# One SBUF offset for weights and tokens, and half of a head pair's scaled states on another engine

## The chip, the cores and the metric

The kernel runs on one core of a Trainium2 chip. The metric is the device time of one execution in microseconds (us). Engines are named as in the profile: PE is TensorE (matmul), PEld its weight load, DVE is VectorE, ACT is ScalarE, POOL is GpSimd, SP is the engine that issues the DMAs.

## The reference: what is computed

Three stages follow each other: a gated linear attention (4 batches, 8 heads, 768 steps, head size 48), a feed-forward layer 384 to 2048 to 384 with `h * cos(h)`, and one 384 to 768 to 384 with the largest of three products. All in float32.

```
for t in range(S):
    state = alpha[:, :, t, :, None] * state + einsum('bhd,bhe->bhde', k[:, :, t], v[:, :, t])
    y[:, :, t] = einsum('bhd,bhde->bhe', q[:, :, t], state)
x = y, as 3072 tokens x 384
h = x @ moe_w_in;  x = (h * cos(h)) @ moe_w_out
h = max(x @ w1, x @ w2, x @ w3);  out = h @ w_out
```

## The kernel before, in words

**Tiling.** The 3072 tokens are cut into 6 units of 512. Tokens lie along the free axis, features along the partitions. Every weight and every token tile is kept as a high and a low part in the format `float32r`, and each product is three matmuls of 128 x 128 weights on 128 x 512 tokens: high times high, high times low, low times high. In the first layer (`moe1`, L489 to L536) one step is one of 16 blocks of 128 hidden features of one unit: nine matmuls into a PSUM bank `ps` (L497 to L499, weights `wih`, `wil`, tokens `xt`), a chain on ACT and DVE that makes `h * cos(h)` and splits it into `gh` and `gl`, and nine matmuls into the three accumulators `acc` (L524 to L526, weights `woh`, `wol`, tokens `gh`, `gl`). There are 96 steps, so 1728 such matmuls. The second layer has `moe2_h` (L574 to L576, weights `w0h` to `w2l`, tokens `xt`) and `moe2_o` (L597 to L599, weights `wo2h`, `wo2l`, tokens `h`), 1296 matmuls of the same shape.

**Attention** (`att`, L337 to L486) works on one pair of heads and one unit, 24 blocks in all, four a unit. The 512 tokens are eight chunks of 64. Per block: scans on DVE make the decays `g` and `al`, two products on POOL scale k and q (`kq`), PE transposes k (L387), makes the scores and the chunk's state increments (L399, L404), DVE runs through the eight chunks' states `s` (L421, L423), each state is scaled by its decay into `d`, and PE makes the values (L449 from the masked scores `a`, L455 from `d`). So each block puts three pieces of small matmuls between the large ones. In the first unit (`u < DAC`) ACT makes `d`, with one ACTIVATE of 48 x 48 per chunk and head of the pair (L430); in the later units POOL does, one TENSOR_TENSOR of 48 x 384 per head (L435).

**Weights.** Each of 32 blocks of the first layer passes through a `raw` buffer (three of them): a DMA, three DVE instructions (L310 to L312), the high part on ACT (L315: `wih`, `woh`), the low part on POOL (L316: `wil`, `wol`). Those of the first layer come in during the first unit.

**The order.** Python records every operation with an engine, an estimated duration, its dependences and a due time. `Program.order` (L118) lays them out on the engines in an imagined run, and picks the PSUM bank of each short-lived tile; the kernel is then issued in that order. Each engine works strictly in its order. So a change of an estimated duration, or of the engine of an operation, moves others on all engines.

**Where tiles lie.** In the built program the token tiles of the first layer (`xt`, `gh`, `gl`) start, within a line of 512 bytes of a partition, at byte 128, and so does each block of 512 or 2048 bytes in them. The first layer's weights are a pool at the other end of SBUF, whose tiles start at byte 480 of such a line. In the second layer `w0h` to `w2l` and `xt` start at byte 128, and `wo2h`, `wo2l` and their tokens `h` at byte 480.

Of the kernel before, what the change touches and what calls it, by code (L numbers as in the profile page):

```python
# [9 lines left out]
F32 = mybir.dt.float32  # L10
# [3 lines left out]
AF = mybir.ActivationFunctionType  # L14
# [4 lines left out]
B, H, S, D = 4, 8, 768, 48  # L19
# [4 lines left out]
P = 128  # L24
C = 64
HB = 512
NC = HB // C
# [4 lines left out]
C1 = C + 1  # L32
AL = NC * C1
N2 = NC // 2
KO = AL + 2
# [5 lines left out]
PR = 112  # L41
# [6 lines left out]


NQ, NG, NRAW, NIN, NV, NGS = 3, 2, 3, 3, 2, 3  # L50
NBANK = 5
LIMIT = {"h": 3, "a": 3, "t": 1, "w": 1, "r": 2, "y": 2, "r0": 4}

# [9 lines left out]
MKP = 1  # L63

DAC = 1


W1E = 10
# [10 lines left out]
class Program:  # L79
# [15 lines left out]
    def op(self, eng, dur, fn, reads=(), writes=(), due=0.0, nbytes=None, port=False):  # L95
        n = len(self.ops)
        deps = set()
        for k in reads:
            if k in self.last_write:
                deps.add(self.last_write[k])  # L100
        for k in writes:
            if k in self.last_write:
                deps.add(self.last_write[k])
            deps.update(self.readers.get(k, ()))
        for k in writes:
            self.last_write[k] = n
            self.readers[k] = []
        for k in reads:
            self.readers.setdefault(k, []).append(n)
        for k in {*reads, *writes}:  # L110
            if isinstance(k, tuple) and k[0] == "ps":
                self.of_bank.setdefault(k, []).append(n)
        deps.discard(n)
        port = port or (eng == "Pool" and nbytes is None)
        self.ops.append((eng, dur, nbytes, fn, sorted(deps), due, port))
        return n
# [89 lines left out]
def act(n, psum=False):  # L206
    return (0.05 if psum else 0.095) + 0.00084 * n
# [6 lines left out]
def pool(n):  # L214
    return 0.16 + 0.0021 * n
# [25 lines left out]
def tile_kernel(ctx, tc, qka, vv, wt, outT):  # L241
    nc = tc.nc
    ve, se, ge, pe = nc.vector, nc.scalar, nc.gpsimd, nc.tensor
# [11 lines left out]
    wp = s_w1.enter_context(tc.tile_pool(name="w1p", bufs=1, side="right"))  # L255
    ap = s_at.enter_context(tc.tile_pool(name="ap", bufs=1))
# [3 lines left out]
    wi = {n: wp.tile([P, NF1, NR, P], F32R, name=f"wi{n}") for n in "hl"}  # L260
    wo = {n: wp.tile([P, NF1, DM], F32R, name=f"wo{n}") for n in "hl"}

    q_b = [mp.tile([P, HB], F32, name=f"q{i}") for i in range(NQ)]
    gh_b = [mp.tile([P, HB], F32R, name=f"gh{i}") for i in range(NG)]
    gl_b = [mp.tile([P, HB], F32R, name=f"gl{i}") for i in range(NG)]
# [2 lines left out]
    acc = [pp.tile([P, HB], F32, name=f"acc{i}") for i in range(NR)]  # L268
    ps_b = [pp.tile([P, 512], F32, name=f"ps{i}") for i in range(NBANK)]

    one0 = ap.tile([PR, NC, C1], F32, name="one0")
    inv0 = [ap.tile([PR, NC, C1], F32, name=f"inv{i}") for i in range(2)]
    tri = ap.tile([P, 1, C], F32, name="tri")
    al_b = [ap.tile([PR, KO], F32, name=f"al{i}") for i in range(NIN)]
    kq_b = [ap.tile([PR, 2 * HB], F32, name=f"kq{i}") for i in range(NIN)]
    g_b = [ap.tile([PR, AL], F32, name=f"g{i}") for i in range(NGS)]
    v_b = [ap.tile([P, N2, 2, UP], F32, name=f"v{i}") for i in range(NV)]
    kt_b = [ap.tile([P, N2, PR], F32, name=f"kt{i}") for i in range(2)]
    a_b = [ap.tile([P, 2, N2, C], F32, name=f"a{i}") for i in range(2)]
# [57 lines left out]
    def att(u, k, p, t0):  # L337
        m = u * NP + k
        n, n2 = m % NIN, m % 2
        t, kq_, v, kt, a, s, d, iv = al_b[n], kq_b[n], v_b[m % NV], kt_b[n2], a_b[n2], s_b[p], d_b[n2], inv0[n2]  # L340
# [8 lines left out]
        g = gf.rearrange("p (c t) -> p c t", c=NC)  # L349
# [4 lines left out]
        kg, ik, tk, dk, sk = ("g", m % NGS), ("iv", n2), ("kt", n2), ("d", n2), ("s", p)  # L354
        firsts = [(u * NC + c) % CPB == 0 for c in range(NC)]
# [3 lines left out]
        if u == 0:  # L359
# [13 lines left out]
            kgs = [(*kg, 0), (*kg, 1)]  # L373
        else:
            op("DVE", 0.07 + 0.00208 * AL, lambda: ve.tensor_tensor_scan(
                gf[:, ::-1], t[:, 1:AL + 1][:, ::-1], one0.rearrange("p c t -> p (c t)"), 0.0, ALU.mult, ALU.add), ["one0", kf], [(*kg, 0), (*kg, 1)], t0 - 1, port=True)
            kgs = [(*kg, 0), (*kg, 1)]
# [40 lines left out]
        def state(c):  # L418
            o, kvc = s[:, (c + 1) % NC], r[c % 2][0:PR, c // 2 * D:(c // 2 + 1) * D]
            if firsts[c]:  # L420
                ve.tensor_copy(o, kvc)  # L421
            else:
                ve.scalar_tensor_tensor(o, s[:, c], g[:, c, 0:1], kvc, ALU.mult, ALU.add)  # L423

        for c in range(NC - 1):
            op("DVE", 0.2, lambda c=c: state(c), [rk[c % 2], *kgs, (*sk, c)], [(*sk, c + 1)], t0 + 0.25)
            if u < DAC and not firsts[c + 1]:
                for j in range(2):
                    w = slice(UP * j, UP * j + D)
                    op("Act", act(D) + 0.09, lambda c=c, j=j, w=w: se.activation(d[w, j, c + 1], s[w, c + 1], AF.Copy, scale=g[w, c + 1, 0:1]),  # L430
                       [*kgs, (*sk, c + 1)], [(dk, j, c + 1)], t0 + 0.25)
        if u >= DAC:
            for j in range(2):
                w = slice(UP * j, UP * j + D)
                op("Pool", pool(NC * D), lambda j=j, w=w: ge.tensor_tensor(d[w, j], s[w], g[w, :, 0:1].to_broadcast([D, NC, D]), ALU.mult),  # L435
                   [*kgs, *[(*sk, c) for c in range(NC)]], [(dk, j, c) for c in range(NC)], t0 + 0.25)
        elif not firsts[0]:
            for j in range(2):
                w = slice(UP * j, UP * j + D)
                op("Act", act(D) + 0.09, lambda j=j, w=w: se.activation(d[w, j, 0], s[w, 0], AF.Copy, scale=g[w, 0, 0:1]), [*kgs, (*sk, 0)], [(dk, j, 0)], t0 + 0.25)  # L440
        op("DVE", 0.2, lambda: state(NC - 1), [rk[1], *kgs, (*sk, NC - 1)], [(*sk, 0)], t0 + 0.27)

        yks, y = ([("acc", 0), ("acc", 1)], acc[:2]) if u == 0 else psum2("r" if u <= RYS else "y")
# [103 lines left out]
    def open_np():  # L547
        s_w1.close()
        np_ = ctx.enter_context(tc.tile_pool(name="np", bufs=1, side="right"))
        w2t["h2"] = [np_.tile([P, NF2, 2, HB], F32R, name=f"h2_{i}") for i in range(2)]  # L550
        w2t["t"] = [np_.tile([P, HB], F32, name=f"t2_{i}") for i in range(2)]
        w2t["y"] = [np_.tile([P, HB], F32, name=f"y2_{i}") for i in range(2)]
        for n in "hl":
            w2t["o" + n] = np_.tile([P, NF2, DM], F32R, name=f"wo2{n}")

    def x2_in(u, t0):
        n = u % 2
        for c in range(NR):
            op("SP", HW, lambda c=c: nc.sync.dma_start(x_tile(NU + u).bitcast(F32)[:, c], x1d[u, c]),
               [("x1d", u, c)] + ([("xtA", n)] if c else []),  # L560
               [*halves(n, c), ("xp", n, c, 0), ("xp", n, c, 1)] + ([] if c else [("xtA", n)]), t0, dma(P * HB * 8))
# [44 lines left out]
    def build():  # L606
# [41 lines left out]
        for u in range(NU):  # L648
            for k, p in enumerate((NP - 1, *range(NP - 1))):
                t = FIRST + k if u == 0 else NF1 * (u - 1) + ATT0 + ATTS * k  # L650
                at(t, att, u, k, p, t)
# [19 lines left out]
        x2_in(0, NS - 8)  # L671
        w1k = [(k, f) for k in ("wih", "wil", "woh", "wol") for f in range(NF1)]
        op("SP", 0.0, open_np, (), w1k + ["np"], NS)
        for f in range(NF2):
            weight(NW1 + 3 * NF2 + f, lambda f=f: w2t["oh"][:, f], lambda f=f: w2t["ol"][:, f],
# [13 lines left out]
    build()  # L689
    order, chosen_ = G.order(NBANK, LIMIT)  # L690
    chosen.update(chosen_)
# [68 lines left out]
```

## Time and profile before

| | |
|---|---|
| median of 3 runs | 831.05 us (829.34 to 832.0) |
| the profiled execution | 831.06 us, span of its instructions 829.3 us |
| PE busy | 805.4 us, 97% of the span |
| DVE, ACT, POOL busy | 477.7 us (58%), 372.5 us (45%), 189.0 us (23%) |
| granted TensorE clock, mean over the span | 0.979 |
| chain that ended last | PE 84%, DVE 5%, POOL 4%, issue 3% |

The busy time of PE counts a matmul from its start to its modelled end, and neighbours overlap: a matmul of 128 x 512 is listed with some 400 ns, while the next one starts much sooner. What a matmul costs in a dense stretch is read from the starts, not from that mean.

### The profile page before, as it was taken

Reading aid. Unit: us, or ns where it says so; the run is one execution under the profiler, and the core shown is the slowest. Engines: PE = TensorE matmul, PEld = TensorE weight load, DVE = VectorE, ACT = ScalarE, POOL = GpSimd, SP = SyncE. Lnnn points to the kernel's source line nnn. Section 1 sums busy time; section 2 is a strip of 40 time slices with the busy share of each in tenths; the row PEclk is TensorE's granted clock in tenths of the full one; section 3 lists DMA queues with packets and bytes.
Section 4 is the critical chain, followed back from the end, with each engine's and each line's share of the span. In section 5 each row is a group of like instructions: output and inputs, shape, how many; then the busy total and the mean of one; then the engine's idle time right before and its main releaser. Section 6 shows DMA issues by size and latency. Waiting matters only on the chain.

```text
span 829.3 us, 15144 instructions
## 1 busy us (share of the span) xinstructions
PE 805.4 (97%) x6168; PEld 649.1 (78%) x6168; DVE 477.7 (58%) x924; ACT 372.5 (45%) x695; POOL 189.0 (23%) x187
## 2 busy tenths in 40 slices
PE   7689999999999999999999999999999999999998
PEld 6567777878778877887788778888888888888886
DVE  7689999875786577657679954453122222322221
ACT  5865655645555554556466745521121211112121
POOL 6478777621231023102033200110000000000000
PEclk8589999999999999999999999999999999999999
DMA  9446764330242024102224610232020020200001
GB/s 281 137 133 193 208 188 150 117 106 12 73 146 65 1 76 143 43 1 74 65 86 134 238 45 2 104 106 77 26 88 19 22 89 25 77 26 13 13 26 38
DMA packets 26661, 71.86 MB, mean 87 GB/s; under 512 B 3488, under 2 KB 3488, under 8 KB 26592
## 3 DMA queue, kind: packets, MB, share of 16 engines
q1 hardware_dynamic: 26592, 70.90, 26.9%
q8 instruction: 48, 0.79, 0.4%
q14 instruction: 21, 0.17, 0.1%
HBM read 54.37 MB, written 14.16 MB: 83 GB/s over the span
## 4 chain that ended last, share of the span: by engine, by line
PE 84%; DVE 5%; POOL 4%; issue 3%; DMA 2%; ACT 1%; SPq 0%; DVEq 0%; POOLq 0%; ACTq 0%
PE ps L575 9%; PE ps L576 9%; PE ps L574 9%; PE acc L524 8%; PE acc L526 7%; PE ps L497 7%; PE acc L525 7%; PE ps L499 7%; PE ps L498 7%; PE ps L599 3%; PE ps L598 3%; PE ps L597 3%; PE ps L455 2%; PE ps L449 1%; PE ps L399 1%
## 5 line engine op out<-in xcount | busy, mean ns | idle before, releaser
L497 PE MATMUL ps<-xt,wih 128*128 128x512 f32 x288 | 117.7, 409 | 2.8 <-ACT q L506 1.7
L524 PE MATMUL acc<-gh,woh 128*128 128x512 f32 x288 | 117.5, 408 | 0.3 <-DVE yy L534 0.2
L499 PE MATMUL ps<-xt,wil 128*128 128x512 f32 x288 | 115.0, 399 | 1.4 <-POOL wil L316 1.4
L526 PE MATMUL acc<-gl,woh 128*128 128x512 f32 x288 | 114.4, 397 | 0.6 <-DVE gl L519 0.4
L498 PE MATMUL ps<-xt,wih 128*128 128x512 f32 x288 | 114.8, 399 | 0.0
L525 PE MATMUL acc<-gh,wol 128*128 128x512 f32 x288 | 114.0, 396 | 0.0
L504 ACT ACTIVATE q<-ps 128x512 int32<-128x512 f32 x96 | 57.2, 596 | 70.8 <-PE ps L499 70.2
L584 DVE TENSOR_TENSOR ps<-t,ps 128x512 f32<-128x512 f32 x36 | 25.0, 695 | 104.8 <-PE ps L576 104.7
L513 DVE SCALAR_TENSOR_TENSOR ps<-q,ps 128x512 f32<-128x512 f32 x76 | 52.7, 693 | 55.4 <-ACT q L507 55.2
L506 ACT ACTIVATE q<-q 128x512 f32<-128x512 f32 x96 | 60.6, 631 | 50.3 <-DVE q L505 49.6
L505 DVE SCALAR_TENSOR_TENSOR q<-q,ps 128x512 f32<-128x512 int32 x96 | 65.8, 685 | 28.0 <-ACT q L504 24.8
L585 ACT ACTIVATE h<-ps 128x512 fp32r<-128x512 f32 x36 | 21.5, 598 | 113.1 <-DVE ps L584 113.0
L519 DVE TENSOR_TENSOR gl<-ps,gh 128x512 fp32r<-128x512 f32 x76 | 52.1, 685 | 26.4 <-ACT gh L514 26.2
L497 PEld LDWEIGHTS ps<-xt,wih 128*128 128x128 f32 x288 | 54.6, 189 | 16.2 <-ACT q L506 2.2
L499 PEld LDWEIGHTS ps<-xt,wil 128*128 128x128 f32 x288 | 54.6, 190 | 15.3 <-POOL wil L316 2.1
L524 PEld LDWEIGHTS acc<-gh,woh 128*128 128x128 f32 x288 | 54.2, 188 | 15.0 <-DVE yy L534 1.1
L582 DVE TENSOR_TENSOR t<-t,ps 128x512 f32<-128x512 f32 x36 | 24.7, 687 | 71.4 <-PE ps L576 70.7
L526 PEld LDWEIGHTS acc<-gl,woh 128*128 128x128 f32 x288 | 54.2, 188 | 14.6 <-DVE gl L519 0.8
L514 ACT ACTIVATE gh<-ps 128x512 fp32r<-128x512 f32 x76 | 45.3, 597 | 42.8 <-DVE ps L513 39.9
L498 PEld LDWEIGHTS ps<-xt,wih 128*128 128x128 f32 x288 | 54.8, 190 | 11.8
L525 PEld LDWEIGHTS acc<-gh,wol 128*128 128x128 f32 x288 | 54.3, 189 | 11.7
L435 POOL TENSOR_TENSOR d<-s,g 48x384 f32<-48x384 f32 x40 | 34.6, 864 | 122.7 <-DVE s L423 121.1
(122 smaller groups left out, 1595.2 us busy)
## 6 DMA issues: line engine op xcount, KB each, us to landing
raw<-in_wt SPq DMA_DIRECT2D x56, 384.0 KB, 3.4
kq<-in_qka SPq DMA_DIRECT2D x23, 448.0 KB, 4.5
x1d<-yy SPq DMA_DIRECT2D x18, 512.0 KB, 2.8
xt<-x1d SPq DMA_DIRECT2D x18, 512.0 KB, 4.3
v<-in_vv SPq DMA_DIRECT2D x22, 256.0 KB, 3.5
al<-in_qka SPq DMA_DIRECT2D x24, 228.4 KB, 3.0
outT<-y SPq DMA_DIRECT2D x18, 256.0 KB, 2.0
xt<-yy SPq DMA_DIRECT2D x36, 64.0 KB, 2.7
```

What stands on the lines that cost most here:

```text
L497: pe.matmul(ps, wi["h"][:, f, cc], xt[:, cc, 0], start=(cc == 0), stop=False)
L498: pe.matmul(ps, wi["h"][:, f, cc], xt[:, cc, 1], start=False, stop=False)
L499: pe.matmul(ps, wi["l"][:, f, cc], xt[:, cc, 0], start=False, stop=(cc == NR - 1))
L504: op("Act", act(HB, True), lambda: se.activation(q.bitcast(I32), ps, AF.Copy, scale=INV2PI), [hk], [qk], m)
L505: op("DVE", dve(HB), lambda: ve.scalar_tensor_tensor(q, q.bitcast(I32), -TWOPI, ps, ALU.mult, ALU.add), [hk], [qk], m)
L506: op("Act", act(HB), lambda: se.activation(q, q, AF.Sin, scale=0.5), (), [qk], m)
L524: pe.matmul(acc[c], oh, gh, start=(f == 0), stop=False)
L525: pe.matmul(acc[c], ol, gh, start=False, stop=False)
L526: pe.matmul(acc[c], oh, gl, start=False, stop=(f == NF1 - 1))
L574: pe.matmul(ps, w2t["h"][m][:, f, cc], xt[:, cc, 0], start=(cc == 0), stop=False)
L575: pe.matmul(ps, w2t["h"][m][:, f, cc], xt[:, cc, 1], start=False, stop=False)
L576: pe.matmul(ps, w2t["l"][m][:, f, cc], xt[:, cc, 0], start=False, stop=(cc == NR - 1))
```

## The change

Three things. First, 352 bytes per partition (`pad`, 88 floats) are added at the end of each of the two pools that lie at the upper end of SBUF, so their tiles move down by 352 bytes: the first layer's weights and the second layer's `h` and `wo2` tiles now start at byte 480 - 352 = 128 of a 512 byte line, as the tokens do. Second, attention's tiles `one0`, `inv`, `al` and `g` are allocated with 544 floats (2176 bytes) and used with their old shapes; the `kq` tiles behind them then start at byte 128 instead of 160, and `v`, `a`, `s` and `d` at byte 0 instead of 256. Third, in the first unit ACT scales only the first head's states; the second head's go to POOL, as in the later units, and the estimated duration of the ACT instruction rises by 0.12 us.

```diff
+PAD = 88
+LINE = 544
+DAH = 1
     wo = {n: wp.tile([P, NF1, DM], F32R, name=f"wo{n}") for n in "hl"}
+    wp.tile([P, PAD], F32, name="pad")
...
-    one0 = ap.tile([PR, NC, C1], F32, name="one0")
+    one0 = ap.tile([PR, LINE], F32, name="one0")[:, 0:AL].rearrange("p (c t) -> p c t", c=NC)
-    al_b = [ap.tile([PR, KO], F32, name=f"al{i}") for i in range(NIN)]
+    al_b = [ap.tile([PR, LINE], F32, name=f"al{i}")[:, 0:KO] for i in range(NIN)]
...
             if u < DAC and not firsts[c + 1]:
-                for j in range(2):
+                for j in range(DAH):
-                    op("Act", act(D) + 0.09, lambda c=c, j=j, w=w: se.activation(d[w, j, c + 1], s[w, c + 1], AF.Copy, scale=g[w, c + 1, 0:1]),
+                    op("Act", act(D) + 0.21, lambda c=c, j=j, w=w: se.activation(d[w, j, c + 1], s[w, c + 1], AF.Copy, scale=g[w, c + 1, 0:1]),
-        if u >= DAC:
-            for j in range(2):
+        for j in range(2):
+            if u >= DAC or j >= DAH:
                 op("Pool", pool(NC * D), lambda j=j, w=w: ge.tensor_tensor(d[w, j], s[w], g[w, :, 0:1].to_broadcast([D, NC, D]), ALU.mult),
                    [*kgs, *[(*sk, c) for c in range(NC)]], [(dk, j, c) for c in range(NC)], t0 + 0.25)
...
         for n in "hl":
             w2t["o" + n] = np_.tile([P, NF2, DM], F32R, name=f"wo2{n}")
+        np_.tile([P, PAD], F32, name="pad2")
```

The order changes on all engines from the first unit on. Lines of the changed file stand 4 or 5 below those of before: L430 is L435 there, L435 is L440, L315 is L320, L470 is L474, L475 is L479. The numbers behind a name are tile numbers, one higher in the changed kernel for most tiles.

ACT before, in the first unit, from the second block's values to the third's (`d_125<-s_122` are the scaled states of the third block, `xt` the copies of finished values):

```order
L475 ACTIVATE yy_89<-acc_95 128x256
L430 ACTIVATE d_126<-s_121,g_113 48x48 x3
L411 ACTIVATE a_119<-ps_99 128x256
L411 ACTIVATE a_119<-ps_98 128x256
L430 ACTIVATE d_125<-s_122,g_114 48x48 x8
L470 ACTIVATE xt_463<-acc_94 128x256
L430 ACTIVATE d_125<-s_122,g_114 48x48
L470 ACTIVATE xt_463<-acc_95 128x256
L430 ACTIVATE d_125<-s_122,g_114 48x48
L475 ACTIVATE xt_463<-acc_94 128x256
L430 ACTIVATE d_125<-s_122,g_114 48x48
```

The same place on ACT in the changed kernel:

```order
L479 ACTIVATE yy_90<-acc_96 128x256
L416 ACTIVATE a_120<-ps_100 128x256
L435 ACTIVATE d_126<-s_123,g_115 48x48
L320 ACTIVATE wih<-raw_92 128x384
L435 ACTIVATE d_126<-s_123,g_115 48x48 x2
L320 ACTIVATE woh<-raw_93 128x384
L435 ACTIVATE d_126<-s_123,g_115 48x48
L474 ACTIVATE xt_451<-acc_95 128x256
L474 ACTIVATE xt_451<-acc_96 128x256
L479 ACTIVATE xt_451<-acc_95 128x256
L435 ACTIVATE d_126<-s_123,g_115 48x48
```

Four scaled states instead of eight stand ahead of the first `xt` copy, and the first two weight blocks, which before came after all of the third block's states, now stand among them.

POOL before, from the third block's products to the fourth's masks (`yy` holds the fourth block's k and q):

```order
L367 TENSOR_TENSOR kq_111<-kq_111,g_114 112x512
L412 TENSOR_TENSOR a_120<-a_120,tri 128x256
L382 TENSOR_TENSOR kq_111<-kq_111,al_108 112x512
L412 TENSOR_TENSOR a_120<-a_120,tri 128x256
L412 TENSOR_TENSOR a_119<-a_119,tri 128x256 x2
L367 TENSOR_TENSOR yy_90<-yy_90,g_112 112x512
L316 TENSOR_TENSOR wil<-raw_91,wih 128x384
L382 TENSOR_TENSOR yy_90<-yy_90,al_106 112x512
L412 TENSOR_TENSOR a_120<-a_120,tri 128x256 x2
```

The same place on POOL in the changed kernel:

```order
L372 TENSOR_TENSOR kq_112<-kq_112,g_115 112x512
L440 TENSOR_TENSOR d_126<-s_125,g_113 48x384
L387 TENSOR_TENSOR kq_112<-kq_112,al_109 112x512
L417 TENSOR_TENSOR a_121<-a_121,tri 128x256 x2
L440 TENSOR_TENSOR d_127<-s_122,g_114 48x384
L417 TENSOR_TENSOR a_120<-a_120,tri 128x256 x2
L321 TENSOR_TENSOR wil<-raw_92,wih 128x384
L321 TENSOR_TENSOR wol<-raw_93,woh 128x384
L372 TENSOR_TENSOR yy_91<-yy_91,g_113 112x512
L440 TENSOR_TENSOR d_126<-s_123,g_115 48x384
L387 TENSOR_TENSOR yy_91<-yy_91,al_107 112x512
```

Three of the four new POOL instructions stand here, and the low parts of the first weights are now ahead of the fourth block's first product instead of between its two products.

## Rows read from the trace of the kernel before

**Rows 1.** The page's parts 1 and 2: busy us (share) xinstructions; granted clock.

```profile
PE 805.4 (97%) x6168; PEld 649.1 (78%) x6168; DVE 477.7 (58%) x924; ACT 372.5 (45%) x695; POOL 189.0 (23%) x187
...
PEclk8589999999999999999999999999999999999999
```

**Rows 2.** Windows: stretch, length, busy us of PE, PEld, DVE, ACT, POOL; clock, DMA.

```profile
20.00:40.00 20.00, 13.82 (x199) 10.90 (x199) 12.31 (x34) 16.11 (x49) 8.71 (x9) 0.50 0.50 135
40.00:120.00 80.00, 72.23 (x798) 56.55 (x799) 74.36 (x158) 49.92 (x99) 62.38 (x55) 0.96 0.60 180
130.00:475.00 345.00, 345.00 (x3254) 275.31 (x3255) 254.29 (x503) 197.66 (x354) 89.67 (x86) 1.00 0.29 89
535.00:829.30 294.30, 290.55 (x1275) 238.90 (x1273) 80.55 (x120) 57.51 (x98) 6.10 (x6) 1.00 0.13 47
```

**Rows 3.** Timeline of PE, its last wait in the first unit: start us, us, [idle before].

```profile
129.88 0.50 PE L526 MATMUL acc<-gl,woh 128*128 128x512 f32 x1 [0.26 <-POOL gl L511]
```

**Rows 4.** Timeline of PE, first and last of 121 `moe1` matmuls in a row.

```profile
499.73 0.40 PE L524 MATMUL acc<-gh,woh 128*128 128x512 f32 x1
...
527.84 0.39 PE L574 MATMUL ps<-xt,w1h 128*128 128x512 f32 x1
```

**Rows 5.** Timeline of PE, first and last of 96 `moe2_h` matmuls in a row.

```profile
603.82 0.39 PE L574 MATMUL ps<-xt,w0h 128*128 128x512 f32 x1
...
625.35 0.39 PE L576 MATMUL ps<-xt,w1l 128*128 128x512 f32 x1
```

**Rows 6.** Timeline of PE, starts of three neighbouring runs of matmuls.

```profile
577.00 0.40 PE L597 MATMUL ps<-h,wo2h 128*128 128x512 f32 x1
...
581.14 0.39 PE L574 MATMUL ps<-xt,w2h 128*128 128x512 f32 x1
...
587.30 0.40 PE L597 MATMUL ps<-h,wo2h 128*128 128x512 f32 x1
```

**Rows 7.** Timeline of PE, first and last matmul of the closing stretch.

```profile
535.48 0.40 PE L574 MATMUL ps<-xt,w2h 128*128 128x512 f32 x1
...
825.16 0.39 PE L599 MATMUL ps<-h,wo2h 128*128 128x512 f32 x1
```

**Rows 8.** Groups of PE's instructions from 130 us on: xcount | busy, mean ns | idle.

```profile
L524 PE MATMUL acc<-gh,woh 128*128 128x512 f32 x248 | 100.9, 407 | 0.3 <-DVE yy L534 0.2
...
L497 PE MATMUL ps<-xt,wih 128*128 128x512 f32 x243 | 98.4, 405 | 0.0
```

**Rows 9.** Groups on ACT and POOL, whole span: the scaled states.

```profile
L435 POOL TENSOR_TENSOR d<-s,g 48x384 f32<-48x384 f32 x40 | 34.6, 864 | 122.7 <-DVE s L423 121.1
...
L430 ACT ACTIVATE d<-s,g 48x48 f32<-48x48 f32 x56 | 18.6, 332 | 1.3
```

**Rows 10.** Timeline of ACT, third and fourth block of the first unit.

```profile
24.32 2.83 ACT L430 ACTIVATE d<-s,g 48x48 f32<-48x48 f32 x8
...
30.68 0.56 ACT L315 ACTIVATE wih<-raw 128x384 fp32r<-128x384 f32 x1
...
37.53 4.97 ACT L430 ACTIVATE d<-s,g 48x48 f32<-48x48 f32 x14
```

**Rows 11.** Timeline of POOL, the same stretch.

```profile
27.14 1.18 POOL L367 TENSOR_TENSOR yy<-yy,g 112x512 f32<-112x512 f32 x1 [1.63 <-DVE g L365]
31.31 2.00 POOL L316 TENSOR_TENSOR wil<-raw,wih 128x384 fp32r<-128x384 f32 x1 [2.99 <-ACT wih L315]
33.27 1.17 POOL L382 TENSOR_TENSOR yy<-yy,al 112x512 f32<-112x512 f32 x1
...
38.42 1.01 POOL L316 TENSOR_TENSOR wol<-raw,woh 128x384 fp32r<-128x384 f32 x1
```

**Rows 12.** Timeline of DVE, the same stretch.

```profile
29.08 0.69 DVE L371 TENSOR_TENSOR_SCAN al<-al,acc 112x260 f32<-112x260 f32 x1
...
30.13 2.37 DVE L375 TENSOR_TENSOR_SCAN g<-al,one 112x520 f32<-112x520 f32 x2
36.97 0.21 DVE L421 COPY s<-ps 112x48 f32<-112x48 f32 x1 [4.47 <-ACT a L411]
```

**Rows 13.** Timeline of PE, the fourth block's scores.

```profile
34.50 1.13 PE L399 MATMUL ps<-yy 48*64 48x64 f32 x32 [1.03 <-POOL yy L382]
```

More of the change, by code (lines that the diff above doesn't have):

```diff
@@ L269, in tile_kernel @@
     ps_b = [pp.tile([P, 512], F32, name=f"ps{i}") for i in range(NBANK)]
-    one0 = ap.tile([PR, NC, C1], F32, name="one0")
-    inv0 = [ap.tile([PR, NC, C1], F32, name=f"inv{i}") for i in range(2)]
+    one0 = ap.tile([PR, LINE], F32, name="one0")[:, 0:AL].rearrange("p (c t) -> p c t", c=NC)
+    inv0 = [ap.tile([PR, LINE], F32, name=f"inv{i}")[:, 0:AL].rearrange("p (c t) -> p c t", c=NC) for i in range(2)]
     tri = ap.tile([P, 1, C], F32, name="tri")
-    al_b = [ap.tile([PR, KO], F32, name=f"al{i}") for i in range(NIN)]
+    al_b = [ap.tile([PR, LINE], F32, name=f"al{i}")[:, 0:KO] for i in range(NIN)]
     kq_b = [ap.tile([PR, 2 * HB], F32, name=f"kq{i}") for i in range(NIN)]
-    g_b = [ap.tile([PR, AL], F32, name=f"g{i}") for i in range(NGS)]
+    g_b = [ap.tile([PR, LINE], F32, name=f"g{i}")[:, 0:AL] for i in range(NGS)]
     v_b = [ap.tile([P, N2, 2, UP], F32, name=f"v{i}") for i in range(NV)]
@@ L436, in att @@
                    [*kgs, *[(*sk, c) for c in range(NC)]], [(dk, j, c) for c in range(NC)], t0 + 0.25)
-        elif not firsts[0]:
-            for j in range(2):
+            elif not firsts[0]:
                 w = slice(UP * j, UP * j + D)
-                op("Act", act(D) + 0.09, lambda j=j, w=w: se.activation(d[w, j, 0], s[w, 0], AF.Copy, scale=g[w, 0, 0:1]), [*kgs, (*sk, 0)], [(dk, j, 0)], t0 + 0.25)
+                op("Act", act(D) + 0.21, lambda j=j, w=w: se.activation(d[w, j, 0], s[w, 0], AF.Copy, scale=g[w, 0, 0:1]), [*kgs, (*sk, 0)], [(dk, j, 0)], t0 + 0.25)
         op("DVE", 0.2, lambda: state(NC - 1), [rk[1], *kgs, (*sk, NC - 1)], [(*sk, 0)], t0 + 0.27)
```

## The prediction

> **What bounds the kernel now.** I read the page's head first: PE is busy for 97% of the span and its clock is at full level but for the first three slices of 20.7 us [rows 1]. [...] The timeline has its last wait of the first unit at 129.88 us [rows 3], and from 130 to 475 us it is busy without a break while DVE has 254 of 345 us and ACT 198. So from 130 us on, what a matmul costs decides, and before that, how soon the first unit's chain is through.
>
> The price of a matmul is read from starts. In `moe1` 120 intervals take from 499.73 to 527.84 us, 234.3 ns each [rows 4]; in `moe2_h` 95 take from 603.82 to 625.35 us, 226.6 ns each [rows 5]. Both groups run at the full clock, have the same shape, and L497 to L499 read the same `xt` tiles and write the same kind of PSUM bank as L574 to L576. What differs is where the weights lie: at byte 480 of a 512 byte line against tokens at 128 in `moe1`, at 128 against 128 in `moe2_h`. That equal bytes and not the byte 128 matter is told by the switches [rows 6]. The 18 matmuls of `moe2_o` (480 against 480) from 577.00 us take 4.14 us and the 27 of `moe2_h` that follow 6.16 us, where 226.6 ns each would make 4.08 and 6.12 us. So both kinds run at the fast price, and after each switch of byte 0.04 to 0.06 us are lost once, while `moe1` pays on every matmul.
>
> **The change part by part.** *Weights at the tokens' byte, first layer.* From 130 us on there are three lines of 243 and three of 248 matmuls [rows 8], 1473 in all. At 234.3 - 226.6 = 7.7 ns each that is 11.3 us, all on the path, since PE has no gaps there and DVE, at 74%, has room for a PE that is 3% faster. Against it stands the price of a switch: the 16 attention blocks of the last four such units put three pieces each between the `moe1` matmuls, with tiles at other bytes, and before now a switch cost `moe1` nothing that it did not pay anyway. 48 switches at 0.05 us would take back 2.4 us, none if the small matmuls do not disturb the pattern; I take half: **10.1 us** gained, between 8.9 and 11.3. Attention's own matmuls change their bytes too. I cost that at nothing: their tiles step through many bytes of a line (chunks of 192, 256 and 448 bytes), so none has one offset before or after. If they did change like `moe1`, by 3.3% either way, it would be on what PE's time between 130 and 535.48 us holds beside 1473 x 0.2343 = 345 us of `moe1` and 24 early matmuls of `moe2_h`: 405.5 - 345 - 5.5 = 55 us, so 1.8 us up or down.
>
> The 220 or so `moe1` matmuls between 60 and 130 us share that stretch with a DVE that is at 93% [rows 2]; a faster PE mostly waits longer there. Of the 1.7 us I take **0.4**.
>
> *Second layer.* With all tiles at byte 128 the switches of rows 6 cost nothing. From 535.48 us to 825.16 us 1272 matmuls start one after the other [rows 7]; 1271 intervals at 226.6 ns make 288.0 us, and 289.68 us pass: **1.6 us** gained, PE being busy for the whole stretch.
>
> *The second head's states on POOL.* ACT loses 28 of its 56 small ACTIVATEs. In a row they take 0.353 us each (eight in 2.83 us, [rows 10]), so 9.9 us of ACT work go; POOL gets four instructions of 0.86 us [rows 9], 3.5 us. What of it is on the path? In the third block ACT works off eleven states, weight block `wih` only comes at 30.68 us, POOL waits 2.99 us for it, takes 2.00 us for the low part, and only then, at 33.27 us, does the fourth block's second product, for which PE waits until 34.50 us [rows 10, 11, 13]. DVE then sits idle for 4.47 us until that block's first state at 36.97 us [rows 12], and DVE is what the next 80 us hang on. The new order puts `wih` and `woh` among the states and their low parts ahead of both products. The second product then waits only for the scan that feeds it, over at 29.77 us even if no scan moves [rows 12]: 33.27 - 29.77 = **3.5 us** earlier. PE is ready by then: the third block's values, which end at 32.4 us now, come 7 x 0.353 = 2.5 us minus what waits for POOL, some 1.9 us, earlier. The new POOL instruction ahead of it (0.86 us) fits between the two products. In the fourth block 14 states take 4.97 us ahead of a weight block [rows 10]; half of that goes and holds the gain. The ends are far apart: a loss of 3.5 us if all four POOL instructions stand in the path, since PE's values of a block now wait for a POOL queue in order, and a gain of 9.9 us if all the ACT time was in it. I take 3.5 because the DVE gap of 4.47 us, the nearest row to what later work hangs on, can give no more than itself.
>
> The move also adds a wait. POOL's instruction reads the whole of `s`, chunk 0 too, so DVE's last state update of a block, which overwrites chunk 0, waits for it. Behind it on DVE stand the next block's states in the first two blocks: about 1 us of delay there, and the next block's scores are not ready much sooner anyway. I count it as covered.
>
> The sum is 10.1 + 0.4 + 1.6 + 3.5 = 15.6 us. The profiled execution took 831.06 us, its span 829.3 us and 1.8 us around it; it stands 0.01 us above the median, so nothing is corrected: 831.1 - 15.6 = **815.5 us**, 810.5 to 819 with the bounds of its terms but for the far ends of the startup.
>
> **The rivals.** *The start gives nothing* (POOL's four instructions eat what ACT gives): 831.1 - 12.1 = 819 us, 817 to 823 if it loses up to 3.5. For it: POOL works in order and is busy for 62 of 80 us later. Against it: in the rows of 20 to 40 us it has 8.7 of 20.
>
> *The start gives much more.* With ACT no longer full (16.1 of 20 us between 20 and 40) and PE's clock at 0.50 there, a denser start could also bring the full clock sooner. 8 us instead of 3.5 and no price for switches: 831.1 - 11.3 - 0.4 - 1.6 - 8 = 810 us, down to 806.
>
> *The place of tiles doesn't count*, and `moe1` is slower for another reason, as more work of the other engines beside it. Then only the start is left: 831.1 - 3.5 = 827.5 us, 823 to 831 us. Against it: the stretches of rows 6 alternate within 2 us without any change beside PE. [...]
>
> *Slower than before: POOL becomes the bound.* The low part of a weight takes 1.01 us alone but 2.00 us when it meets DVE's scan of two SBUF tiles [rows 11, 12]. From 40 to 120 us POOL has 17.6 us to spare and 55 instructions [rows 2]. If the new order made them meet the scans more often, each would cost 1.0 us; beyond 18 such meetings the chain of weights is late, and beyond 30 the 12.1 us from the matmuls are gone. With 40: 831 - 12 + 22 = 841 us. For it: all orders move. Against it: such scans come two to a block after the first unit, so some ten in that stretch, and ten cannot meet 30 instructions. [...]
>
> **How the numbers follow.** Forecast 0.55, start gives nothing 0.20, start gives more 0.14, place doesn't count 0.08, POOL the bound 0.03. About 0.3% (2.5 us) is what a measurement of this kernel can tell from no change. Faster by more than that are the first three and half of the fourth: 0.93. Within it 0.035, slower 0.035. The range of 8 in 10 takes the forecast, nearly all of the second case and two thirds of the third: 808 to 822 us.
>
> **What would show it.** Right: dense stretches of `moe1` with starts 227 ns apart, and some nine matmuls after an attention piece a little above; 1271 closing intervals in 288.0 us; in the first unit L435 x28 on ACT, L440 x44 on POOL at 0.86 us, DVE's gap before the fourth block's first state at 1 us or less, that state at 33 to 34 us. Wrong: `moe1` still at 234 ns; settling after each piece for far more than nine matmuls; gaps on PE beyond 130 us with DVE or POOL as releaser; the first `xt` copies later than before.

## The result: 816.8 us, and the profile after

The changed kernel takes 816.79 us (median of 4 runs, 815.08 to 820.0) against 831.0 us for the kernel before in the same session: a ratio of 0.9835, with a 95% interval of 0.9801 to 0.987, so 14.2 us less. Forecast were 815.5 us, between 808 and 822. The profiled execution took 816.9 us, its span is 815.2 us. It is read here by the stretches of [rows 2]. Two runs of the experiments below that lie far above the others of the same kernel, 888.9 us with the two pads alone (the one with the trace) and 1577.5 us with the padded tiles alone, are left out of their times.

**The page.** Parts 1 and 2 of the changed kernel's page, the counterpart of [rows 1]:

```profile
PE 791.5 (97%) x6168; PEld 646.0 (79%) x6168; DVE 476.4 (58%) x924; ACT 360.9 (44%) x667; POOL 192.8 (24%) x191
...
PEclk8789999999999999999999999999999999999999
```

PE has the same 6168 instructions and is busy 13.9 us less; that is nearly the whole gain. ACT has 28 instructions less and POOL four more.

**By stretch.** Windows over the changed kernel (length; busy us of PE, PEld, DVE, ACT, POOL; clock, DMA), the counterpart of [rows 2]:

```profile
20.00:40.00 20.00, 14.01 (x264) 11.11 (x263) 17.90 (x42) 11.64 (x35) 15.44 (x15) 0.75 0.72 216
40.00:120.00 80.00, 71.77 (x750) 56.28 (x750) 74.49 (x162) 50.20 (x98) 64.36 (x56) 0.96 0.55 171
130.00:475.00 345.00, 343.95 (x3277) 278.04 (x3276) 255.26 (x503) 200.51 (x361) 84.41 (x82) 1.00 0.29 90
523.00:811.10 288.10, 288.10 (x1273) 238.55 (x1271) 80.15 (x120) 57.01 (x97) 6.13 (x6) 1.00 0.13 48
```

In the first stretch DVE is busy 17.9 instead of 12.3 us and POOL 15.4 instead of 8.7, ACT only 11.6 instead of 16.1, and PE's clock there is 0.75 instead of 0.50: the start is denser. From 40 to 120 us little differs. From 130 to 475 us PE is busy for 343.95 of 345 us, and the closing stretch is shorter.

**`moe1`.** PE's timeline in the changed kernel, one run of 102 `moe1` matmuls between two attention pieces (start us, us):

```profile
250.02 0.99 PE L459 MATMUL ps<-kq,d 112*48 112x64 f32 x28
250.94 0.50 PE L528 MATMUL acc<-gh,woh 128*128 128x512 f32 x1
251.27 0.40 PE L529 MATMUL acc<-gh,wol 128*128 128x512 f32 x1
...
253.11 0.39 PE L501 MATMUL ps<-xt,wih 128*128 128x512 f32 x1
...
273.96 0.39 PE L503 MATMUL ps<-xt,wil 128*128 128x512 f32 x1
```

From 253.11 to 273.96 us 92 intervals pass, 226.6 ns each, where [rows 4] had 234.3 (120 `moe1` matmuls; the last row there is already the first matmul of the second layer). From the second matmul (251.27) to 253.11 us there are eight intervals of 230 ns on average: the run needs some seven matmuls after the attention piece before it has the low price.

**The second layer.** First and last matmul of the closing stretch, the counterpart of [rows 7]:

```profile
522.99 0.39 PE L579 MATMUL ps<-xt,w2h 128*128 128x512 f32 x1
...
811.09 0.39 PE L604 MATMUL ps<-h,wo2h 128*128 128x512 f32 x1
```

The same 1271 intervals take 288.10 instead of 289.68 us, 226.7 ns each.

**The start.** Four timelines of the changed kernel at the fourth block, the counterparts of [rows 11], [rows 10], [rows 12] and [rows 13]. POOL:

```profile
21.91 1.03 POOL L321 TENSOR_TENSOR wil<-raw,wih 128x384 fp32r<-128x384 f32 x1
...
24.18 1.17 POOL L372 TENSOR_TENSOR yy<-yy,g 112x512 f32<-112x512 f32 x1
25.43 0.85 POOL L440 TENSOR_TENSOR d<-s,g 48x384 f32<-48x384 f32 x1
26.38 1.18 POOL L387 TENSOR_TENSOR yy<-yy,al 112x512 f32<-112x512 f32 x1
```

ACT, the first of these weight blocks and the third block's last scaled states:

```profile
21.22 0.57 ACT L320 ACTIVATE wih<-raw 128x384 fp32r<-128x384 f32 x1
...
24.86 0.69 ACT L435 ACTIVATE d<-s,g 48x48 f32<-48x48 f32 x2
```

DVE, the block's first state, and PE, its scores and the first `moe1` matmul:

```profile
30.77 0.21 DVE L426 COPY s<-ps 112x48 f32<-112x48 f32 x1 [0.98 <-ACT a L416]
```

```profile
28.28 1.13 PE L404 MATMUL ps<-yy 48*64 48x64 f32 x32
...
32.04 0.47 PE L501 MATMUL ps<-xt,wih 128*128 128x512 f32 x1 [1.28 <-DMA xt<-yy]
```

The low parts now stand ahead of both products and take 1.03 us instead of 2.00, the second product starts at 26.38 instead of 33.27 us, the scores at 28.28 instead of 34.50, the first state at 30.77 instead of 36.97, with 0.98 us of idle DVE ahead of it instead of 4.47. The groups that answer to [rows 9], on ACT and on POOL (busy, mean ns, idle before):

```profile
L435 ACT ACTIVATE d<-s,g 48x48 f32<-48x48 f32 x28 | 9.0, 332 | 2.1 <-DVE s L428 1.4 <-DVE s L426 0.4
```

```profile
L440 POOL TENSOR_TENSOR d<-s,g 48x384 f32<-48x384 f32 x44 | 37.0, 842 | 125.5 <-DVE s L428 123.7
```

The fourth block is 6.2 us earlier, but the end of the start is not. PE's timeline some 20 us later:

```profile
49.93 0.39 PE L503 MATMUL ps<-xt,wil 128*128 128x512 f32 x1
53.36 0.64 PE L392 MATMUL ps<-ident,kq 112*128 112x112 f32 x4 [3.04 <-DVE raw L317]
53.86 0.79 PE L501 MATMUL ps<-xt,wih 128*128 128x512 f32 x1
54.45 0.63 PE L502 MATMUL ps<-xt,wih 128*128 128x512 f32 x1
...
57.31 0.40 PE L503 MATMUL ps<-xt,wil 128*128 128x512 f32 x1
```

PE's transposes wait 3.04 us for the last of the three DVE instructions that unpack a weight block. They read no weight: what the two can share in the program is a PSUM bank, which the transposes write and in which DVE unpacks the block (that it was one bank is not shown). Behind that idle time the `moe1` matmuls from 54.45 to 57.01 us start 427 ns apart, at a granted clock of 0.50.

**Where the 14 us are.** The matmuls that start from 130 us on, summed from start to start without waits, with their mean:

| | before | after |
|---|---|---|
| `moe1` | 1473 in 352.87 us, 239.6 ns | 1454 in 340.12 us, 233.9 ns |
| second layer | 1295 in 295.37 us | 1295 in 293.69 us |
| attention | 2008 in 46.07 us | 2008 in 45.99 us |

The lower price of a `moe1` matmul is worth 1454 x 5.65 ns = 8.2 us. The start is worth the 19 matmuls that are done before 130 us now, 19 x 0.2396 = 4.6 us, less 0.4 us of longer waits behind 130 us. The second layer gives 1.7 us (1.58 of it in the closing stretch), attention 0.1. Together, before rounding, these are 14.1 us; the last matmul starts 14.07 us earlier.

### The profile page after: what moved, and what is told of

It is laid out like the page before. It is cut to its first block, busy times and chain, and to the rows that moved or that the text cites. A ratio compares the mean times of both kernels' runs of the same rounds, so it can differ in the third digit from the quotient of the medians.

```text
span 815.2 us, 15114 instructions
## 1 busy us (share of the span) xinstructions
PE 791.5 (97%) x6168; PEld 646.0 (79%) x6168; DVE 476.4 (58%) x924; ACT 360.9 (44%) x667; POOL 192.8 (24%) x191
## 4 chain that ended last, share of the span: by engine, by line
PE 84%; DVE 6%; POOL 4%; issue 2%; DMA 2%; ACT 2%; SPq 0%; POOLq 0%; DVEq 0%; ACTq 0%
PE ps L580 9%; PE ps L579 9%; PE ps L581 9%; PE acc L528 7%; PE ps L501 7%; PE acc L530 7%; PE acc L529 7%; PE ps L503 7%; PE ps L502 7%; PE ps L603 3%; PE ps L602 3%; PE ps L604 3%; PE ps L459 2%; PE ps L404 1%; PE ps L453 1%
## 5 line engine op out<-in xcount | busy, mean ns | idle before, releaser
L501 PE MATMUL ps<-xt,wih 128*128 128x512 f32 x288 | 116.3, 404 | 3.7 <-ACT kt L395 2.2
L502 PE MATMUL ps<-xt,wih 128*128 128x512 f32 x288 | 113.2, 393 | 0.0
L503 PE MATMUL ps<-xt,wil 128*128 128x512 f32 x288 | 113.0, 392 | 0.0
L440 POOL TENSOR_TENSOR d<-s,g 48x384 f32<-48x384 f32 x44 | 37.0, 842 | 125.5 <-DVE s L428 123.7
```

The lines of the kernel that those rows point to most:

```text
L501: pe.matmul(ps, wi["h"][:, f, cc], xt[:, cc, 0], start=(cc == 0), stop=False)
L502: pe.matmul(ps, wi["h"][:, f, cc], xt[:, cc, 1], start=False, stop=False)
L503: pe.matmul(ps, wi["l"][:, f, cc], xt[:, cc, 0], start=False, stop=(cc == NR - 1))
```

## The experiments

The theory was the prediction's: two independent gains, the offset of weights to tokens (A and B of what follows: first and second layer) and the denser start (C). The rivals were that the estimates and the order alone make the difference, that the padding of attention's tiles plays a part, and that something other than the offset sets a matmul's price.

**Only the two pads.** The kernel before, with the same order:

```diff
+    wp.tile([P, PAD], F32, name="pad")
...
+        np_.tile([P, PAD], F32, name="pad2")
```

> The kernel before with the two pads of 352 bytes alone: attention's tiles, the split of the scaled states and the order are those of before. If the byte of weights and tokens sets a matmul's price: dense moe1 starts 226.6 ns apart, the closing stretch without switch costs, 11 to 12 us faster than before (ratio 0.985 to 0.987), and the first unit as before (fourth block's first state at 37 us). If the price comes from the new order or from attention's tiles: 234 ns and a ratio of 1.00.

Measured: 821.5 us, 0.988 of before [0.9863, 0.9897], so 10.2 us faster, a little less than the 11 to 12 us expected. Only its time is used, so that its dense `moe1` stretches run at 226.6 ns is not shown by this run itself. The rival, 1.00, is out: the two pads alone give 10.2 us without any change of order.

**Only the start.** The other half: second head to POOL and the new ACT estimate, no pad and no padded tiles.

```diff
-                for j in range(2):
+                for j in range(DAH):
...
-        if u >= DAC:
-            for j in range(2):
+        for j in range(2):
+            if u >= DAC or j >= DAH:
```

> The changed kernel's split of the scaled states and its new ACT estimate, so its whole order, without the pads and with attention's tiles as before. If the start is a term of its own: the fourth block's first state at 31 us as in the changed kernel, dense moe1 at 234 ns, 2.5 to 4 us faster than before (ratio 0.995 to 0.997). If the earlier start was only good because PE was faster behind it: ratio 0.999 to 1.00.

Measured: 827.5 us, 0.9958 [0.9944, 0.9973], 4.2 us faster. In its trace 1457 `moe1` matmuls remain from 130 us on, 16 fewer than before, at 239.7 ns against 239.6 before: 16 x 0.2396 = 3.8 us. The fourth block's first state stands at 30.95 us there, as expected. The two halves make 14.4 us, and the whole change 14.2: within the intervals they add.

**Only attention's padded tiles.**

```diff
-    g_b = [ap.tile([PR, AL], F32, name=f"g{i}") for i in range(NGS)]
+    g_b = [ap.tile([PR, LINE], F32, name=f"g{i}")[:, 0:AL] for i in range(NGS)]
```

(likewise `one0`, `inv`, `al`)

> The kernel before with attention's tiles of 544 floats alone. The order is that of before; only the bytes of attention's tiles move. If attention's small matmuls don't care for their bytes, as I costed it: ratio 1.000, attention's pieces as long as before. If they do: the pieces change by up to 3.3%, 2 us either way (0.998 to 1.002).

Measured: 831.68 us, 1.0001 [0.9991, 1.0011]. This part of the change does nothing.

**Only the ACT estimate.** 0.21 instead of 0.09 for the small ACTIVATEs, both heads still on ACT:

```diff
-                    op("Act", act(D) + 0.09, ...
+                    op("Act", act(D) + 0.21, ...
```

> The kernel before with the ACT estimate 0.12 us higher and nothing else: ACT still scales both heads' states, in the order that the higher estimate gives. If the start is won by taking work off ACT: within 1.5 us of before (0.998 to 1.002). If it is won by an order that knows ACT's true price: 2 to 4 us faster (0.995 to 0.9975), and the split adds nothing.

Measured: 838.74 us, 1.0086 [1.007, 1.0101], 7 us slower; both theories missed that. PE's longest waits in that kernel (us in total, times, longest):

```profile
PE acc L449 <- POOL a L412: 5.5, 5, 2.8
PE ps L497 <- DMA xt<-yy: 2.9, 1, 2.9
```

and its window from 20 to 54 us:

```profile
20.00:54.00 34.00, 23.79 (x310) 18.37 (x310) 29.03 (x64) 24.65 (x71) 21.82 (x22) 0.51 0.60 170
```

PE's granted clock is 0.51 over the stretch, against 0.60 before, and the first `moe1` matmul starts at 43.61 us instead of 36.75. The estimate is truer, 0.345 us in all instead of 0.225 where [rows 9] has 0.332, but the order is worse: with ACT still full (15.76 of the 20 us from 20 us on), the plan moved work to where PE waits for it, POOL's masks (L412) above all.

**The old estimate with the split.** The changed kernel with 0.09 in place of 0.21:

```diff
-op("Act", act(D) + 0.21, ...
+op("Act", act(D) + 0.09, ...
```

> The changed kernel with the old estimate for the scaled states on ACT (0.12 us lower): half of them still go to POOL, the order is planned with the low price. If the split alone shortens the start: within 1.5 us of the changed kernel (0.982 to 0.985). If the split needs an order that knows ACT's price: 2 to 5 us slower than the changed kernel (0.986 to 0.99).

Measured: 817.75 us, 0.9831 [0.9818, 0.9845], the changed kernel's time. So what the start gains comes from the split, the work that leaves ACT, and does not need the new estimate.

**Both heads to POOL.** The changed kernel with no scaled state of the first unit on ACT:

```diff
-DAH = 1
+DAH = 0
```

> The changed kernel with both heads' scaled states of the first unit on POOL. If ACT's queue is what the start still hangs on: 1 to 3 us faster than the changed kernel (0.98 to 0.982). If POOL's queue then holds PE's values, as I feared of the change itself: 1 to 4 us slower (0.985 to 0.988).

Measured: 822.99 us, 0.9899 [0.9883, 0.9915], 5 to 6 us slower than with one head and more than the 1 to 4 us that were feared. Its PE, the fourth block's scores and the start of `moe1`:

```profile
28.49 1.13 PE L404 MATMUL ps<-yy 48*64 48x64 f32 x32 [0.93 <-POOL yy L387]
...
34.55 0.39 PE L477 MATMUL acc<-xt,minus 128*128 128x256 f32 x1 [1.93 <-ACT xt L474]
34.77 0.39 PE L501 MATMUL ps<-xt,wih 128*128 128x512 f32 x1
```

its POOL at that place,

```profile
28.51 1.66 POOL L440 TENSOR_TENSOR d<-s,g 48x384 f32<-48x384 f32 x1
31.31 1.42 POOL L417 TENSOR_TENSOR a<-a,tri 128x256 f32<-128x256 f32 x2 [1.14 <-ACT a L416]
```

and its first stretch:

```profile
20.00:40.00 20.00, 16.10 (x305) 13.43 (x298) 17.27 (x43) 8.02 (x21) 17.86 (x18) 0.61 0.65 192
```

POOL is busy for 17.86 of 20 us, ACT for 8.02: the full queue has moved from ACT to POOL. With one head neither queue is full (POOL 15.44, ACT 11.64 us). PE's waits for POOL's second product (us in total, times, longest), with one head and with none on ACT:

```profile
PE ps L404 <- POOL kq L387: 1.9, 3, 0.8
```

```profile
PE ps L404 <- POOL kq L387: 4.7, 3, 2.5
```

That PE can come to wait for POOL, the prediction's slower rival, is real, though not yet with the four instructions of the change. These waits make 2.8 us of the 5 to 6; the rest was not told apart.

**The second pad left out.** The changed kernel, with `h` and `wo2` at byte 480 again:

```diff
-        np_.tile([P, PAD], F32, name="pad2")
```

> The changed kernel without the pad of the second layer's pool, whose tiles then start at byte 480 again. If the switch of bytes between moe2_h and moe2_o is what the second layer paid: its closing 1271 intervals take 1.4 to 1.6 us longer than in the changed kernel, 0.985 to 0.9855 of before in all. If not: as the changed kernel, 0.9835.

Measured: 818.81 us, 0.9843 [0.9822, 0.9864]. 2 us are too little for the intervals to tell; its closing stretch tells:

```profile
523.42 0.39 PE L578 MATMUL ps<-xt,w2h 128*128 128x512 f32 x1
...
813.06 0.39 PE L603 MATMUL ps<-h,wo2h 128*128 128x512 f32 x1
```

289.64 us for 1271 intervals, as in [rows 7], against 288.10 with the pad: B is 1.54 us and comes from this pad, which takes away the switches of [rows 6].

**The offset by itself.** A program of matmuls alone, which computes nothing of the reference: 20 stretches of 63 matmuls of the kernel's shape and kind, with four weight blocks and two token blocks in turn, each stretch at another pair of byte offsets:

```
    for i in range(63):
        pe.matmul(ps[i // 9 % 2], w(i, 352), x(i, 0), start=i % 9 == 0, stop=i % 9 == 8)
```

> Not the kernel but its matmul alone: stretches of 63 matmuls of 128 x 128 weights on 128 x 512 tokens, four weight blocks and two token blocks in turn, each stretch at another pair of bytes of weights and tokens within 512; it computes none of the reference and writes one tile everywhere. If equal bytes are what counts: 226.6 ns at every pair of equal bytes (0 and 0, 352 and 352, 128 and 128, 64 and 64) and 234 ns at the pair 352 and 0 that the kernel before had; unequal pairs nearby are open, 226.6 to 240 ns. If the absolute byte of the weights counts: 352 and 352 stays at 234 ns. If the place doesn't count: one price.

PE's timeline, whole stretches (start, length). The offsets of weights and tokens are, from L266 on: (0,0), (352,0), (4,0), (16,0); L280 is (192,0), L282 (256,0), L284 (320,0), L288 (448,0), L290 (480,0), L292 (508,0), L294 (352,352):

```profile
25.84 14.44 PE L266 MATMUL ps<-X,W 128*128 128x512 f32 x63
40.12 14.91 PE L268 MATMUL ps<-X,W 128*128 128x512 f32 x63
54.87 14.80 PE L270 MATMUL ps<-X,W 128*128 128x512 f32 x63
69.52 14.86 PE L272 MATMUL ps<-X,W 128*128 128x512 f32 x63
...
128.26 14.86 PE L280 MATMUL ps<-X,W 128*128 128x512 f32 x63
142.96 14.46 PE L282 MATMUL ps<-X,W 128*128 128x512 f32 x63
157.26 14.86 PE L284 MATMUL ps<-X,W 128*128 128x512 f32 x63
...
186.59 14.59 PE L288 MATMUL ps<-X,W 128*128 128x512 f32 x63
201.02 14.85 PE L290 MATMUL ps<-X,W 128*128 128x512 f32 x63
215.71 14.44 PE L292 MATMUL ps<-X,W 128*128 128x512 f32 x63
229.99 14.50 PE L294 MATMUL ps<-X,W 128*128 128x512 f32 x63
```

From one start to the next, 63 intervals: 14.28 us or 226.7 ns at equal offsets (L266), 14.75 us or 234.1 ns at 352 bytes apart (L268), 14.43 us or 229.0 ns at 448. No other engine has work here, and (352,0) is as far apart as weights and tokens of `moe1` were before, so its price there is the offset and nothing beside PE. Nor is it the weights' own place: (352,352) has the low price again but for 0.06 us in all (L294, 14.50 us long against 14.44 of L266). But 256 bytes apart costs nothing (L282, 14.30 us), and neither do weights 4 bytes behind (L292, 14.28 us). So the two need not agree modulo 512 bytes, as the change has it. Nor is the place modulo 256 the whole rule: 192 and 448 bytes are equal by it and take 233.3 and 229.0 ns (L280, L288).

**256 bytes apart in the kernel.** The changed kernel with the pads at 24 floats: all weights of the first layer, and `h` and `wo2`, at byte 384, the tokens at 128.

```diff
-PAD = 88
+PAD = 24
```

> The changed kernel with both pads 24 floats instead of 88: the weights of the first layer, and h and the second layer's right-side tiles, then lie at byte 384 of a 512-byte line while xt, which both layers read, stays at 128, so 256 bytes apart. Theory 'equal modulo 256': the probe had 226.7 ns both for 0 and for 256 bytes between the two operands, so dense moe1 stretches again take 226.7 ns, the closing stretch of 1271 intervals 288.1 us, and the time is that of the changed kernel, 0.983 to 0.986 of before. Rival 'equal modulo 512', on which the change was built: dense moe1 at 232 to 234 ns, 1473 x 7 ns = 10 us lost again, time about 0.995.

Measured: 817.09 us, 0.9823 [0.9808, 0.9838], the changed kernel's time. The run that was shown above for the changed kernel, here from its tenth matmul to its last:

```profile
252.47 0.39 PE L501 MATMUL ps<-xt,wih 128*128 128x512 f32 x1
...
273.32 0.39 PE L503 MATMUL ps<-xt,wil 128*128 128x512 f32 x1
```

92 intervals of 226.6 ns. That 256 bytes apart cost nothing holds in the kernel too.

**Attention's other tiles moved.** The changed kernel with 32 floats more ahead of `v`, `kt`, `a`, `s` and `d`, which then start at byte 128 of a line:

```diff
+    ap.tile([P, 32], F32, name="pad3")
```

> The changed kernel with 32 more floats ahead of attention's tiles v, kt0, a, s and d, so that they start at byte 128 of a line like q, k, the tokens and the weights. Theory 'settling is a change of offset': attention's pieces then disturb the pattern less, the matmuls 1 to 7 after a piece fall from 230-237 ns towards 227, 45 pieces x 38 ns = 1.6 us at most are gained, 0.981 to 0.984. Rival 'any piece of small matmuls disturbs it, since its tiles step through many bytes': the positions 1 to 7 stay at 230 to 237 ns and the time stays within 0.7 us of the changed kernel.

Measured: 816.79 us, 0.982 [0.9805, 0.9835]. Behind the same attention piece:

```profile
249.11 0.40 PE L530 MATMUL acc<-gh,wol 128*128 128x512 f32 x1
...
250.95 0.39 PE L502 MATMUL ps<-xt,wih 128*128 128x512 f32 x1
```

Eight intervals in 1.84 us, 230 ns, exactly as in the changed kernel. Moving these tiles by 128 bytes does not change the settling. A change of offset alone can cost as much as a switch in [rows 6]: in the probe, with no small matmul between, the 63 intervals at (352,352), right behind those at (508,0), take 14.34 us (L296 starts at 244.33 us), 0.06 us more than the 14.28 at (0,0). Whether attention's small steps add to that stays open.

**A truer price for a matmul in the planner.**

```diff
-    return (n + 0.375 * m) / 2400.0
+    return (n + 0.25 * m) / 2400.0
```

> The changed kernel with only the planner's estimate of a matmul changed, (n + 0.25 m)/2400 instead of (n + 0.375 m)/2400: 226.7 ns for a 128x512 one, which is what a dense stretch now takes, instead of 233.3. Theory 'the planner's numbers matter little': it places the same work in slightly other orders, within 1.5 us of the changed kernel, 0.982 to 0.986. Rival 'the two new small PE gaps and the 3.0 us gap at 53.4 us come from a plan that takes PE for slower than it is': 1.5 to 4 us faster than the changed kernel, 0.979 to 0.982, with the gap at 53 us below 2 us. The run with the other ACT estimate alone (7 us slower) warns of a third way: a worse start, 0.986 or more.

Measured: 819.07 us, 0.9856 [0.9835, 0.9877], by its median 2.3 us behind the changed kernel, with intervals that overlap. The wait at 53 us is gone, as the rival had it, and the start is better: before 130 us PE waits at most 1.9 us at a time, and 291 `moe1` matmuls start there instead of 274, which is worth 17 x 0.234 = 4.0 us. But at the end of `moe1` stands

```profile
466.14 0.80 PE L528 MATMUL acc<-gh,woh 128*128 128x512 f32 x1 [3.27 <-DVE yy L538]
```

where the changed kernel waits 0.51 us at 466.06 us; from 466.73 to 471.43 us the matmuls behind it start some 427 ns apart, the spacing that the changed kernel had from 54.45 to 57.01 us at a granted clock of 0.50. The longer wait, 2.8 us, and these 11 intervals, 0.2 us each too long, take the 4.0 us back and more. None of the versions is measurably faster than the changed kernel.

## Why the prediction was right, step by step

**What bounds the kernel.** Right: from 130 us on only the price of a matmul decided, and DVE, ACT and POOL did not become late when PE became faster. PE's waits beyond 130 us in the changed kernel are two:

```profile
PE acc L528 <- DVE yy L538: 0.5, 1, 0.5
PE acc L530 <- DVE gl L523: 0.4, 1, 0.4
```

They stand at the change from the first layer to the second, where before 0.2 and 0.4 us were lost.

**First layer: the mechanism right, the size too large.** The term said 10.1 us, between 8.9 and 11.3; 8.2 us were measured. The gain of a matmul in a dense run is as stated, 7.7 ns. What was too small is the price of a switch. The text took half of 48 x 0.05 us, 1.2 us. In the trace there are 45 pieces; the matmuls at positions 1 to 6 behind them cost 1.5 us more than 226.7 ns each would, and the matmul right at an edge gains less than 7.7 ns: 293.1 ns against 299.5 ahead of a piece, 330.8 against 332.5 behind it, 0.3 us lost. So some 1.8 us are paid, three quarters of the 2.4 and not half. Further than twelve matmuls from attention, intervals at least 15 ns above the dense price number 9 with 1.1 us instead of 5 with 0.6: 0.5 us of small stalls, whose cause was not looked for. Some 0.7 us more that are missing to 1454 x 7.7 ns = 11.2 us were not told apart. The 0.4 us for the matmuls before 130 us can't be told apart from the start. The pads alone gave 10.2 us where these two terms and the second layer's made 12.1.

**Second layer: right.** 1.6 us forecast, 1.58 measured between the rows, 1.54 taken back when the pad is left out.

**The start: right, by a chain that moved further than forecast.** 3.5 us forecast, 4.2 measured. The order of causes was as told: low parts ahead of both products at 1.0 us, the product earlier, DVE's gap below 1 us. But the product came 6.9 us earlier instead of 3.5, since the scan that feeds it moved too: the text let it end at 29.77 us, and the product now runs from 26.38, and the fourth block's first state stood at 30.77 us, not at 33 to 34: 6.2 us earlier, more than the 4.47 us of DVE's gap, which the text took for the most that the place can give. What made the sum come out is that a part was given back, by the 3.04 us wait at 53.36 us and the granted clock of 0.50 behind it: the 20th `moe1` matmul starts 5.3 us earlier than before, the 40th 2.8, the 250th 3.7. The prediction had no term for that. The choice of 3.5 was closer than its reason.

**The covered wait of DVE** behind POOL's read of `s`: right as far as the total shows. DVE's waits for POOL's scaled states make 0.3 us in the changed kernel and 0.3 us with all states on POOL, where PE's waits for POOL grow instead.

**Attention's tiles at nothing: right**, 46.07 to 45.99 us, and nothing by themselves.

**The sum.** 15.6 us were forecast and 14.2 measured. The first layer gave 1.9 us less than its term, the start 0.7 us more, for a reason that was not the text's. That the total lies 1.3 us from the forecast is in this part luck.

**The rivals.** *The start gives nothing* falls with the run of the start alone, *the place doesn't count* with the run of the pads alone and with the probe, whose neighbouring stretches of the same instructions take 226.7 and 234.1 ns (L266, L268; mean granted clock of that run 0.979). *POOL the bound* did not happen; PE's waits for POOL's second product grow from 1.9 to 4.7 us with twice the added work on POOL. *The start gives much more*, 8 us, did not happen either: 4.2.

## What to carry to other kernels

Compare the start-to-start time of the same matmul in different stages: 3% between two dense stretches at a granted clock of 1.00 (234.3 against 226.6 ns) came here from where weights and tokens lie against each other, and a pad of 352 bytes, which puts both at the same byte of a 512 byte line, or of 96, which puts them 256 bytes apart, took it away. Small pieces with other tiles in between cost some seven matmuls of settling each here (230 ns on average against 226.6), so the full gain comes only in long runs. Where a planner orders the work, a better estimate is a change of order like any other: one alone cost 7 us here, and only moving work off the full engine paid.

## What the runs showed of the hardware that was not expected

- The price of a matmul depends on how far its weights lie ahead of its tokens: 226.7 ns at 0, 227.0 at 256 bytes (226.6 in the kernel with pads of 24 floats), 229.0 at 448, 232 to 234 at the others tried, but 226.7 again at 508 bytes, which is 4 bytes behind. A difference of 4 bytes the other way (L270) costs 14.65 us / 63 = 232.5 ns. No rule that covers all of these was found; each offset of the probe was tried once, in one run.
- Idle time of 3.04 us on PE was followed by 3.15 us at a granted clock of 0.50, 53.86 to 57.01 us, so that place cost more than the wait's length: the eight matmuls from 53.86 to 57.31 us take 3.45 us, where 8 x 0.227 makes 1.8.
- The low part of a weight on POOL takes 1.03 us in its new place and 2.00 us beside a scan of DVE with two inputs in SBUF [rows 11, 12]; where it stood in the order doubled it here.
